# Attention and token-mixing on one core: eight changes in a hand-written order of steps

## The chip, the cores and the metric

The kernel runs on one core of a Trainium2 chip. The metric is the device time of one execution in microseconds (us); lower is better. A core has five engines that each work through their own list of instructions in order and meet only through semaphores: PE (TensorE, matrix products and transposes, with weight loads shown as PEld), DVE (VectorE), ACT (ScalarE), POOL (GpSimd) and SP (SyncE), which here only issues DMA transfers.

## What is computed

```python
# q, k, v: (8, 8, 576, 64) f32; per batch b and head h
r = relu(x);  phi(x) = concat([r * cos_w, r * sin_w], -1)      # 64 -> 128 features
kv  = einsum('bhsf,bhsd->bhfd', phi(k), v);  z = sum_s phi(k)
x   = (phi(q) @ kv) / (phi(q) @ z + 1e-6)                      # (8, 576, 512) with heads side by side
wq  = x @ w_q;  wk = x @ w_k                                   # (8, 576, 64)
W   = einsum('bsd,btd->bst', wq, wk) / 8
out = relu(einsum('bst,btd->bsd', W, x)) @ w_out               # (8, 576, 512) f32
```

The kernel computes the token mix as `wq @ (wk' x)`, so that the 576 x 576 matrix is never made.

## The kernel before

All work is cut into small named steps. A string, `ORDER`, lists some 650 of them, and a loop at the end of the kernel calls one function per word. The order on each engine is therefore the order of that engine's words in the list; nothing reorders it. The framework adds the waits between engines from the data that the steps read and write, on-chip memory banks included. SP's list is that of the loads (`LK`, `LQ`, `LV`, `LW`) and stores (`ST`): a store that waits for its data holds up every load written behind it.

A word is a step's name, a number, perhaps `a` or `b` for one half of it, `:n` for the PSUM bank, and `@A`, `@V` or `@G` for ACT, DVE or POOL. PSUM, the only memory that PE writes, has eight banks. Most steps write a pair, `n` and `n + 1`; `WK`, `WQ`, `KX` and `WO` write one. A step that writes a bank has to wait until the step that read the bank's former content is done. This reuse couples the engines most around the change.

The 64 (batch, head) pairs are worked on as 16 halves `H` of four heads (two pairs of heads each); a half gives two groups `g` = 2H and 2H + 1 (one head of each pair). For one half:

- `LK`, `LQ`, `LV` (line 145): load k, q and v, in parts a and b of 288 KB. Five buffers for each, so half 5 reuses those of half 0.
- `RK`, `RQ` (lines 203 and 205): relu and cast to bf16. `CV`, `VS` (lines 209 to 213 and 234) or, on POOL alone, `VG` (line 248): v times the cosine and sine tables.
- `QT` (wide: line 295, narrow: line 301) transposes q on PE: nine 128 x 128 transposes if the half is in `QT_WIDE`, else eighteen of 64 rows. `QM` (lines 316 and 320) multiplies the transposed q by the tables on DVE: two instructions for a wide half, one for a narrow one.
- `KV` (line 285, or wide: line 275) forms k'v with the sum of k in an extra column; `KE` copies it out of PSUM.
- `N` (line 340) is the numerator and denominator of one group; `EP`, `RC` or `RJ` and `X` (lines 357 to 393) divide and store x.
- `XT` (line 406) or `XR` (line 419) transposes x on PE, `XE` copies it out.

For a batch `b` of two halves: `WK` (line 439), `KW`, `WQ` (line 452), `QW`, `KX` (line 466), `XK` are the two projections and `wk' x`, with their copies; `XA` and `XB` copy one half of `wk' x` to the other 64 partitions, for each half of the channels. `MX` (line 489) gives the mixed tokens, four steps for a batch, and `ME` (lines 500 and 502) applies relu. Every nine `WO` (line 509) multiply two batches by w_out, 128 rows each; `OE` (lines 209 and 213) copies a result to one of 16 output buffers and `ST` (line 519) stores it.

In the trace all casts and copies of ACT have line 209, those of POOL line 211 and those of DVE line 213, so a row is matched with a step by its shape, its tile names and its place in the engine's order. For example the bank pairs around the two places in the middle read so:

```
PE: XR6:0 WO1:6 WO4:2 QT9:0 WK3:3 QT8:4 KV8:0 KV9:6 MX9:4 MX11:0 N16:2
PE: WO11:0 WO5:1 WO10:4 WO9:5 QT11:6 KV11:2 XR8:0 XR9:6 QT10:2 WO0:5 MX13:0 MX12:6 N22:2
PE: QT12:0 WO16:2 WO13:3 XR10:4 MX19:6 KV12:0 WO17:3 MX17:0 N25:6 N24:4
```

Of the kernel before, what the change touches and what calls it, by code (L numbers as in the profile page):

```python
# [26 lines left out]
LK1b TB TI LQ1a LQ0a TK LV1b TZ LV1a LK1a LQ1b TQ LQ0b LK0a RQ1a@G LV0a TW TV LV0b LK0b CV1@A LV3a
LV3b VS1b RQ1b@A LQ3b VS1a T2 QT1:0 LQ3a RK1a@A RK1b@V RQ0@V LK3b KV1:2 QM1 LK3a QT0:4 KE1@A CV0@G
LV2b RK0@A LW1 N2:2 VS0 N3:0 LQ2a LK2a VG3 QM0 KV0:6 LW0 KE0@A LV2a RC3 EP2@A X3 RQ3@A N0:6 N1:4
LQ2b RC2 EP0@V EP1@V X2 RK3@A LK2b QT3:0 RC0 XT1:2 LV5b X0 LV5a XE1@A RC1 X1 VG2b KV3:6 QM3 LK5b  # L30
XR0:4 KE3@A CW1@A N6:0 LK5a LQ5a XE0@V EP6@A N7:6 CW0@G LQ5b EP7@A WK0:4 VG2a RQ2@A LQ4b WQ0:5 KW0@V
RC6 LQ4a KX0:4 X6 RK2@A QT2:2 RC7 X7 CV5@A KV2:0 LK7a XK0@V LV4a QM2 XB0@G QW0@A XT3:6 LV4b KE2@A
RK5@A LK4a VS5a N5:0 WU5:2 LK4b N4:2 VS5b XE3@A RQ5@G LV7a EP5@V KV5:4 RC5 RC4 X5 XA0@A LV7b X4
QT5:6 KE5@A RQ4@G LQ7b MX0:0 QM5 XR2:2 ME0@A LQ7a QT4:4 XE2@A LQ6a N10:0 QM4 MX1:6 CV4@G LK7b EP10@A
ME1@A WK1:2 LV6b WQ1:3 RC10 KW1@A VS4 RK4@A LQ6b KX1:2 MX2:6 LW2 N11:4 XK1@V QW1@A ME2@A EP11@V
KV4:2 LK6b RC11 XA1@G X10 CV7a@A CV7b@G LK6a X11 MX5:6 MX4:0 KE4@A RQ7b@G LV6a RQ7a@A VS7 N8:2 N9:4
ME5@A LV8a ME4@A QT7:6 RK7@G LW3 EP8@V EP9@V RJ4 RQ6a@A XT5:0 X8 LW4 XB1@G XE5@A X9 KV7:2 LW5 RQ6b@G
QM7 LQ8b VG6b MX6:4 KE7@A XT4:0 LQ9b ME6@A MX7:2 XE4@V QT6:6 LV8b ME7@A N15:4 QM6 RK6a@A LQ8a MX3:2
N14:0 CV6a@G EP15@A RK6b@A WK2:6 LV9b ME3@A VS6a WQ2:7 LK8a KW2@A RC14 KV6:2 RC15 QW2@A LQ9a X14
CV8a@G KX2:7 LV9a KE6@A CW4@G X15 CW2@A N13:2 LK9a CW3@A CW5@V N12:0 EP13@V XR7:4 XK2@V LK8b WO8:6  # L40
RC13 XA2@A X13 EP12@A CV8b@G LK9b XE7@A WO2:7 RC12 VS8 LV11a WO7:2 CV9b@A RQ8a@G X12 OE8:0@A MX8:4
WO6:3 RQ8b@A RK8a@G LQ13a ME8@V OE7:1@A LQ11b XR6:0 RQ9a@G LQ10a WO1:6 CV9a@A XE6@V RQ9b@G LK11b
OE2:2@A WO4:2 LK11a VS9 OE6:3@A LQ11a RK8b@A QT9:0 RK9a@G OE1:4@A WK3:3 LV11b QM9 QT8:4 RK9b@G KW3@A
OE4:5@A KV8:0 QM8 XB2@A KV9:6 ST4 KE8@A LV12a MX9:4 KE9@A MX11:0 VG11a N16:2 ME9@A LK10a ME11@V
WQ3:6 RC16 LQ10b KX3:7 X16 QW3@A MX10:0 LV10a XK3@A N17:4 ME10@A N19:2 RK11@V N18:6 LV10b EP19@A
WO11:0 EP17@V RQ11@A LQ12a RC17 EP18@V X17 WO5:1 VG11b OE11:6@V WO10:4 OE5:5@A RC19 RC18 ST11 X18
WO9:5 LK12a X19 LK10b QT11:6 LQ13b OE9:7@A RQ10@G LV12b KV11:2 XA3@A QM11 XR8:0 LK12b KE11@A XR9:6
VG10a XE8@A QT10:2 LQ12b XE9@V WO0:5 QM10 OE10:8@A MX13:0 OE0:6@A MX12:6 N22:2 WO12:4 RQ13a@G ME12@V
EP22@A LV15a XB3@A ME13@A LV13a RC22 VG10b WK4:5 X22 LQ14b LV14b MX14:0 KW4@A N23:6 ME14@V LQ14a
MX15:2 EP23@A KX4:5 RK10@A LV13b WQ4:0 XK4@V RQ13b@G RC23 WO3:1 ME15@A X23 XA4@G XB4@A QW4@A RQ12b@G  # L50
KV10:2 OE3:9@V RQ12a@A QT13:6 OE12:10@A VG12 MX18:0 WO14:5 QM13 KE10@A ST12 ME18@A LK13b XR11:2
OE14:11@A LK13a MX16:0 N21:6 XE11@V ME16@A LV14a N20:4 EP21@A EP20@V RK12@A QT12:0 RJ10 X21 WO16:2
RQ14b@A X20 WO13:3 QM12 VG13 XR10:4 OE13:10@A MX19:6 KV12:0 ME19@A ST13 WO17:3 OE16:12@A LK15b
KE12@V XE10@V LK14b MX17:0 LK14a OE17:13@A N25:6 ME17@V N24:4 LV15b RQ14a@A WK5:3 ST2 EP25@V EP24@V
RK13@A RJ12 QT14:0 X24 WO21:2 KW5@A X25 CV14a@G KV13:4 OE21:10@A QM14 CV14b@A WQ5:3 ST21 KE13@A
# [2 lines left out]
ME23@A OE20:10@V XR13:4 RQ15a@G MX22:6 RQ15b@V MX20:0 ST20 ME22@A WO15:2 VG15a ST17 XE13@V ME20@A
ST8 N28:6 OE18:9@V OE15:14@A ST9 N29:0 EP28@A QT15:4 RK15@A EP29@V RC28 WK6:3 RC29 X29 WO25:2 KW6@A
QM15 WQ6:3 OE25:15@A KV15:0 X28 QW6@A ST25 ST7 KX6:3 KE15@A ST15 N31:0 ST18 XR14:6 EP31@V N30:4 ST0  # L60
XE14@V WO23:2 EP30@A ST10 XK6@A RJ15 ST16 X30 XA6@G WO24:3 ST5 OE23:7@A XB6@G X31 WO26:2 OE24:0@A
ST14 XR15:0 ST6 MX25:4 MX27:6 XE15@V ME25@A WO22:3 ST23 ME27@V ST1 WK7:0 OE26:9@V ST24 MX24:6 KW7@A
MX26:4 WQ7:1 ME24@A ME26@V ST19 KX7:0 OE22:8@V ST26 WO28:2 XK7@A QW7@V ST22 XA7@G WO27:3 OE28:11@A
XB7@G ST28 MX31:0 MX28:4 MX30:6 ME31@V ME28@A WO29:2 ME30@A OE27:7@V MX29:4 OE29:4@V WO30:0 ME29@A
ST27 ST29 WO32:1 OE30:2@V WO33:4 ST30 OE32:9@V WO34:0 ST32 OE33:8@A WO35:1 ST33 OE34:7@V WO31:4 ST34
OE35:4@A ST35 OE31:2@A ST31
"""


# [1 line left out]
def kernel(  # L71
# [240 lines left out]
    def QM(H, ps, eng):  # L312
        if H in QT_WIDE:
            q_t = qt_wide(place["QT", H]).rearrange("p c (r d) -> p r c d", r=2)
            for r in range(2):
                V.tensor_mul(  # L316
                    qm_b[H % NQM][:, :, r, 0:C, :],
                    q_t[:, r].unsqueeze(1).to_broadcast([P, 2, C, H2]), qtab)
# [280 lines left out]
```

## Time and profile before

| | |
|---|---|
| three runs | 119.94, 120.47, 120.84 us; median 120.47 |
| span of the profiled execution, first to last instruction | 117.9 us |
| its own time | not recorded beside the profile; the median is 2.57 us above its span |
| mean granted PE clock | 0.997 |
| busy: PE, DVE, ACT, POOL | 96.3, 91.0, 82.7, 64.8 us |
| moved by DMA | 39.38 MB, mean 334 GB/s |

An engine's busy time is the time in which at least one of its instructions was running. A row of a timeline gives start, duration, engine, source line, operation, output and inputs with their shapes, and the number of like instructions in a row that were merged; in brackets stands the time that the engine sat idle just before, and what released it, as far as the profile can infer it. The rows of PE overlap a little, since matmuls are pipelined and their ends are modelled; from start to start is the surer measure. Idle time on an engine that is not the bottleneck costs nothing.

### The profile page before, as it was taken

Reading aid. Unit: us, or ns where it says so; the run is one execution under the profiler, and the core shown is the slowest. Engines: PE = TensorE matmul, PEld = TensorE weight load, DVE = VectorE, ACT = ScalarE, POOL = GpSimd, SP = SyncE. Lnnn points to the kernel's source line nnn. Section 1 sums busy time; section 2 is a strip of 40 time slices with the busy share of each in tenths; the row PEclk is TensorE's granted clock in tenths of the full one; section 3 lists DMA queues with packets and bytes.
Section 4 is the critical chain, followed back from the end, with each engine's and each line's share of the span. In section 5 each row is a group of like instructions: output and inputs, shape, how many; then the busy total and the mean of one; then the engine's idle time right before and its main releaser. Section 6 shows DMA issues by size and latency. Waiting matters only on the chain.

```text
span 117.9 us, 4967 instructions
## 1 busy us (share of the span) xinstructions
PE 96.3 (82%) x2109; PEld 65.3 (55%) x2109; DVE 91.0 (77%) x163; ACT 82.7 (70%) x146; POOL 64.8 (55%) x66
## 2 busy tenths in 40 slices
PE   0007866887897879998999889997999999999970
PEld 0006855756676768546966556654784566463420
DVE  2009799699899998989798887796997996794620
ACT  4555578489999797997684769975888783546340
POOL 7600599843435984584599972899549921102000
PEclk9999999999999999999999999999999999999998
DMA  3999999999999999999999899786989456999874
GB/s 95 353 389 408 393 363 351 391 389 396 385 393 389 391 385 387 389 395 384 387 381 341 271 317 379 274 253 215 299 285 321 171 205 268 402 343 402 340 306 172
DMA packets 20662, 39.38 MB, mean 334 GB/s; under 512 B 3232, under 2 KB 3232, under 8 KB 20640
## 3 DMA queue, kind: packets, MB, share of 16 engines
q1 hardware_dynamic: 20640, 39.07, 91.8%
q8 instruction: 16, 0.26, 1.0%
q14 instruction: 6, 0.05, 0.1%
HBM read 29.62 MB, written 9.44 MB: 331 GB/s over the span
## 4 chain that ended last, share of the span: by engine, by line
PE 46%; DMA 25%; DVE 9%; SPq 8%; ACT 4%; issue 3%; POOL 2%; POOLq 0%; DVEq 0%
PE ps L509 23%; DMA kraw<-in_k_dram 11%; DMA vraw<-in_v_dram 9%; SPq L145 8%; DMA qraw<-in_q_dram 5%; DVE qm L316 5%; PE ps L340 4%; PE ps L452 3%; PE ps L466 3%; PE ps L489 3%; PE ps L439 3%; PE ps L285 3%; PE ps L419 2%; PE ps L295 2%; POOL rq L205 2%
## 5 line engine op out<-in xcount | busy, mean ns | idle before, releaser
L248 POOL TENSOR_TENSOR v<-vraw,vtab 128x1152 bf16<-128x1152 f32 (+1 forms) x12 | 35.6, 2976 | 4.5 <-DVE qm L316 2.5
L509 PE MATMUL ps<-wow,mix 128*128 128x512 bf16 x144 | 34.6, 380 | 0.0
L393 DVE TENSOR_TENSOR x<-ps,rec 128x640 bf16<-128x640 f32 x32 | 25.4, 816 | 0.7
L209 ACT COPY o<-ps 128x512 f32<-128x512 f32 x25 | 14.6, 590 | 10.5 <-PE ps L509 9.2
L316 DVE TENSOR_TENSOR qm<-ps,qtab 128x1152 bf16<-128x1152 bf16 x28 | 19.7, 749 | 1.3 <-PE ps L295 1.2
L509 PEld LDWEIGHTS <-mix 128*128 128x128 bf16 x144 | 12.5, 98 | 14.5 <-issue 1.7
L295 PE MATMUL ps<-ident,rq 128*128 128x128 bf16 x126 | 10.3, 232 | 10.9 <-ACT rq L203 10.0
L234 DVE TENSOR_TENSOR v<-vb,vtab 128x2304 bf16<-128x2304 bf16 (+1 forms) x11 | 12.0, 1110 | 7.5 <-ACT vb L209 6.7
L500 ACT ACTIVATE mix<-ps 128x576 bf16<-128x576 f32 x23 | 14.5, 651 | 2.5 <-PE ps L489 2.3
L340 PE MATMUL ps<-kvs,qm 64*128 64x65 bf16 x640 | 14.0, 193 | 2.8 <-DVE qm L316 1.8
L340 PEld LDWEIGHTS <-qm 64*128 64x128 bf16 x640 | 12.6, 96 | 4.9 <-issue 3.3
L295 PEld LDWEIGHTS <-rq 128*128 128x128 bf16 x126 | 8.2, 104 | 12.5 <-issue 9.9
L203 ACT ACTIVATE rk<-kraw 128x1152 bf16<-128x1152 f32 (+1 forms) x14 | 13.9, 995 | 0.5 <-DMA kraw<-in_k_dram 0.3
L211 POOL TENSOR_SCALAR kx<-kx 64x256 bf16<-64x256 bf16 x10 | 4.0, 400 | 15.8 <-ACT kx L209 10.1
L205 POOL TENSOR_SCALAR rq<-qraw 128x576 bf16<-128x576 f32 (+1 forms) x13 | 10.1, 776 | 4.4 <-ACT rk L203 2.6
L211 POOL TENSOR_SCALAR vb<-vraw 128x576 bf16<-128x576 f32 (+1 forms) x7 | 5.7, 809 | 10.8 <-DMA vraw<-in_v_dram 9.5
L285 PE MATMUL ps<-v,rk 64*64 64x130 bf16 x432 | 9.1, 228 | 1.9 <-ACT mix L500 0.7
L209 ACT CAST kvs<-ps 128x260 bf16<-128x260 f32 (+1 forms) x15 | 6.5, 436 | 5.1 <-PE ps L285 3.8
L285 PEld LDWEIGHTS <-rk 64*64 64x64 bf16 x432 | 7.5, 112 | 4.3 <-ACT mix L500 1.3
L502 DVE TENSOR_SCALAR mix<-ps 128x576 bf16<-128x576 f32 x9 | 6.8, 753 | 3.3 <-PE ps L489 3.1
L213 DVE COPY xT<-ps 128x1280 bf16<-128x1280 bf16 (+1 forms) x9 | 7.3, 813 | 2.2 <-PE ps L419 2.0
L203 ACT ACTIVATE rq<-qraw 128x576 bf16<-128x576 f32 (+1 forms) x10 | 8.3, 830 | 0.9 <-DMA qraw<-in_q_dram 0.8
(65 smaller groups left out, 135.0 us busy)
## 6 DMA issues: line engine op xcount, KB each, us to landing
kraw<-in_k_dram SPq DMA_DIRECT2D x32, 288.0 KB, 5.9
qraw<-in_q_dram SPq DMA_DIRECT2D x32, 288.0 KB, 5.9
vraw<-in_v_dram SPq DMA_DIRECT2D x32, 288.0 KB, 5.9
out_dram<-o SPq DMA_DIRECT2D x36, 256.0 KB, 3.0
wof<-in_moe_w_out_dram SPq DMA_DIRECT2D x4, 256.0 KB, 5.7
wkf<-in_moe_w_k_dram SPq DMA_DIRECT2D x1, 128.0 KB, 6.7
wqf<-in_moe_w_q_dram SPq DMA_DIRECT2D x1, 128.0 KB, 6.5
```

Source lines behind the costliest of these rows:

```text
L203: A.activation(dst, s, AF.Relu)
L205: eng.tensor_scalar(dst, s, FMAX, 0.0, op0=ALU.min, op1=ALU.max)
L209: A.copy(dst, s)
L234: V.tensor_mul(v2_b[H % NV2][:, part, :, :, 0:D], vb_b[H % NPREP][:, part].unsqueeze(3).to_broadcast([P, n, C, 2, D]), vtab.unsqueeze(1).t ...
L248: G.tensor_mul(dst[:, part, :, :, 0:D], s[:, part].unsqueeze(3).to_broadcast([P, n, C, 2, D]), vtab.unsqueeze(1).to_broadcast([P, n, C, 2, ...
L285: nc.tensor.matmul(kv_v[o, r, :], rk_of(H)[a, pr, c, :], v2_b[H % NV2][a, pr, c, :, 0:D + 1], start=(c == 0), stop=(c == C - 1))
L295: nc.tensor.transpose(qt_v[:, c, :], rq_b[H % NPREP][:, c, :, :], ident)
L316: V.tensor_mul(qm_b[H % NQM][:, :, r, 0:C, :], q_t[:, r].unsqueeze(1).to_broadcast([P, 2, C, H2]), qtab)
L340: nc.tensor.matmul(nv[:, pr, u, :], qm_b[H % NQM][a, s, r, 2 * u:2 * u + 2, :], kv_b[H % 2][a, r, pr if H in KV_WIDE else 0, s, 0:D + 1], ...
L393: V.tensor_tensor(x_b[b % NX][:, :, 4 * h:4 * h + 4, :].rearrange("p u (w r) d -> p r w u d", r=2)[:, r], nv[:, :, :, 0:D], rec(g).to_broa ...
L500: A.activation(dst, s, AF.Relu, scale=scale_moe)
L509: nc.tensor.matmul(o, mix_b[bp % 2][:, m, rt * P:(rt + 1) * P], wow[:, m, :], start=(m == 0), stop=(m == NDM - 1))
```

## The change

`ORDER` is written anew, and almost every line of the list differs, since loads and stores stand in other columns between the same neighbours of their own queue. What matters is each engine's own order. There it does the following; DVE's order stays as it is.

```diff
 SP
-LQ0b LK0a LV0a LV0b LK0b LV3a
+LQ0b LV0a LV0b LK0b LK0a LV3a
 PE
-XR6:0 WO1:6 WO4:2 QT9:0 WK3:3 QT8:4 KV8:0
+XR6:0 WO1:6 QT8:4 QT9:0 WK3:3 WO4:2 KV8:0
...
-WO11:0 WO5:1 WO10:4 WO9:5 QT11:6 KV11:2 XR8:0 XR9:6 QT10:2
+WO11:0 WO5:1 QT11:4 WO9:0 WO10:1 KV11:2 XR8:6 XR9:4 QT10:2
...
-XR10:4 MX19:6 KV12:0 WO17:3
+XR10:4 KV12:6 MX19:0 WO17:3
...
-WO25:2 WQ6:3 KV15:0 KX6:3 N31:0
+WO25:2 KV15:0 KX6:3 WQ6:2 N31:0
 ACT
-QW1@A ME2@A CV7a@A KE4@A
+QW1@A ME2@A XA1@A CV7a@A KE4@A
...
-OE25:15@A QW6@A KE15@A EP30@A
+OE25:15@A KE15@A QW6@A EP30@A
 POOL
-CV4@G XA1@G CV7b@G
+CV4@G CV7b@G
```

The other edit is in the list of the wide halves, which half 12 leaves:

```diff
-    QT_WIDE = (0, 1, 2, 3, 4, 5, 6, 7, 8, 9, 10, 11, 12, 14)
+    QT_WIDE = (0, 1, 2, 3, 4, 5, 6, 7, 8, 9, 10, 11, 14)
```

So half 0's first part of k is loaded three places later; two q transposes stand ahead of output products, one k'v ahead of a mix product, and with them the banks of seven steps are exchanged; one projection stands behind `wk' x`; one small copy changes its engine; and the transposes of half 12 are eighteen narrow ones, with one `QM` instruction instead of two.

More of the change, by code (lines that the diff above doesn't have):

```diff
@@ L26 @@
 ORDER = """
[L27 to L55, printed above, removed]
@@ L56 @@
-KX5:2 LQ15b VS14 LQ15a XR12:4 XK5@A N27:0 ST3 XE12@A N26:6 LK15a RK14a@G WO20:2 RC26 EP27@V RC27
-XA5@G RK14b@A X27 WO19:4 XB5@G QW5@A VG15b X26 KV14:0 OE19:2@A MX21:6 KE14@A MX23:4 WO18:3 ME21@V
[L58 to L66, printed above, removed]
+LK1b LQ1a LQ0a LV1b LV1a LK1a LQ1b LQ0b LV0a LV0b LK0b LK0a LV3a LV3b LQ3b LQ3a LK3b LK3a LV2b LW1
@@ new lines @@
+LQ2a LK2a LW0 LV2a LQ2b LK2b TB TI TK TZ TQ RQ1a@G TW TV CV1@A VS1b RQ1b@A VS1a T2 QT1:0 RK1a@A
+RK1b@V RQ0@V KV1:2 QM1 QT0:4 KE1@A CV0@G LV5b LV5a RK0@A LK5b LK5a LQ5a LQ5b LQ4b LQ4a N2:2 VS0 N3:0
+VG3 QM0 KV0:6 KE0@A RC3 EP2@A X3 RQ3@A N0:6 N1:4 RC2 EP0@V EP1@V X2 RK3@A QT3:0 RC0 XT1:2 X0 XE1@A
+RC1 X1 VG2b KV3:6 QM3 XR0:4 KE3@A CW1@A N6:0 XE0@V EP6@A N7:6 CW0@G EP7@A WK0:4 VG2a RQ2@A WQ0:5
+KW0@V RC6 KX0:4 X6 RK2@A LK7a LV4a LV4b LK4a LK4b LV7a LV7b LQ7b LQ7a LQ6a LK7b LV6b LQ6b LW2 LK6b
+LK6a LV6a LV8a LW3 LW4 LW5 LQ8b QT2:2 RC7 X7 CV5@A KV2:0 XK0@V QM2 XB0@G QW0@A XT3:6 KE2@A RK5@A
@@ new lines @@
+VS5a N5:0 WU5:2 N4:2 VS5b XE3@A RQ5@G EP5@V KV5:4 RC5 RC4 X5 XA0@A X4 QT5:6 KE5@A RQ4@G LQ9b LV8b
+LQ8a MX0:0 QM5 XR2:2 ME0@A QT4:4 XE2@A N10:0 QM4 MX1:6 CV4@G LV9b LK8a LQ9a LV9a EP10@A ME1@A WK1:2
+WQ1:3 RC10 KW1@A VS4 RK4@A LK9a LK8b LK9b KX1:2 MX2:6 N11:4 XK1@V QW1@A ME2@A EP11@V KV4:2 XA1@A
+RC11 X10 CV7a@A CV7b@G X11 MX5:6 MX4:0 KE4@A RQ7b@G RQ7a@A VS7 N8:2 N9:4 ME5@A ME4@A QT7:6 RK7@G
+EP8@V EP9@V RJ4 RQ6a@A XT5:0 X8 XB1@G XE5@A X9 KV7:2 RQ6b@G QM7 VG6b MX6:4 KE7@A XT4:0 ME6@A MX7:2
+XE4@V QT6:6 ME7@A N15:4 QM6 RK6a@A MX3:2 N14:0 CV6a@G LV11a EP15@A RK6b@A WK2:6 ME3@A VS6a WQ2:7
@@ new lines @@
+KW2@A RC14 KV6:2 RC15 QW2@A X14 CV8a@G KX2:7 KE6@A CW4@G X15 CW2@A N13:2 CW3@A CW5@V N12:0 EP13@V
+XR7:4 XK2@V WO8:6 RC13 XA2@A X13 EP12@A CV8b@G XE7@A WO2:7 RC12 VS8 WO7:2 CV9b@A RQ8a@G LQ13a LQ11b
+LQ10a LK11b LK11a LQ11a LV11b X12 OE8:0@A MX8:4 WO6:3 RQ8b@A RK8a@G ME8@V OE7:1@A XR6:0 RQ9a@G WO1:6
+CV9a@A XE6@V RQ9b@G OE2:2@A QT8:4 VS9 OE6:3@A RK8b@A QT9:0 RK9a@G OE1:4@A WK3:3 QM9 WO4:2 RK9b@G
+KW3@A OE4:5@A ST4 LV12a LK10a LQ10b LV10a LV10b LQ12a KV8:0 QM8 XB2@A KV9:6 KE8@A MX9:4 KE9@A MX11:0
@@ new lines @@
+VG11a N16:2 ME9@A ME11@V WQ3:6 RC16 KX3:7 X16 QW3@A MX10:0 XK3@A N17:4 ME10@A N19:2 RK11@V N18:6
+EP19@A WO11:0 EP17@V RQ11@A RC17 EP18@V X17 WO5:1 VG11b OE11:6@V ST11 LK12a LK10b LQ13b LV12b LK12b
+LQ12b QT11:4 OE5:5@A RC19 RC18 X18 WO9:0 X19 WO10:1 OE9:7@A RQ10@G KV11:2 XA3@A QM11 XR8:6 KE11@A
+XR9:4 VG10a LV15a LV13a LQ14b LV14b LQ14a LV13b XE8@A QT10:2 XE9@V WO0:5 QM10 OE10:8@A MX13:0
+OE0:6@A MX12:6 N22:2 WO12:4 RQ13a@G ME12@V EP22@A XB3@A ME13@A RC22 VG10b WK4:5 X22 MX14:0 KW4@A
+N23:6 ME14@V MX15:2 EP23@A KX4:5 RK10@A WQ4:0 XK4@V RQ13b@G RC23 WO3:1 ME15@A X23 XA4@G XB4@A QW4@A
@@ new lines @@
+RQ12b@G KV10:2 OE3:9@V RQ12a@A QT13:6 OE12:10@A ST12 LK13b LK13a LV14a VG12 MX18:0 WO14:5 QM13
+KE10@A ME18@A XR11:2 OE14:11@A MX16:0 N21:6 XE11@V ME16@A N20:4 EP21@A EP20@V RK12@A QT12:0 RJ10 X21
+WO16:2 RQ14b@A X20 WO13:3 QM12 VG13 XR10:4 OE13:10@A ST13 LK15b LK14b LK14a LV15b ST2 KV12:6 MX19:0
+ME19@A WO17:3 OE16:12@A KE12@V XE10@V MX17:0 OE17:13@A N25:6 ME17@V N24:4 RQ14a@A WK5:3 EP25@V
+EP24@V RK13@A RJ12 QT14:0 X24 WO21:2 KW5@A X25 CV14a@G KV13:4 OE21:10@A ST21 LQ15b LQ15a ST3 LK15a
+QM14 CV14b@A WQ5:3 KE13@A KX5:2 VS14 XR12:4 XK5@A N27:0 XE12@A N26:6 RK14a@G WO20:2 RC26 EP27@V RC27
@@ new lines @@
+XA5@G RK14b@A X27 WO19:4 XB5@G QW5@A VG15b X26 KV14:0 OE19:2@A MX21:6 KE14@A MX23:4 WO18:3 ME21@V
+ME23@A OE20:10@V ST20 ST17 ST8 ST9 XR13:4 RQ15a@G MX22:6 RQ15b@V MX20:0 ME22@A WO15:2 VG15a XE13@V
+ME20@A N28:6 OE18:9@V OE15:14@A N29:0 EP28@A QT15:4 RK15@A EP29@V RC28 WK6:3 RC29 X29 WO25:2 KW6@A
+QM15 OE25:15@A ST25 ST7 ST15 ST18 ST0 ST10 ST16 ST5 ST14 ST6 KV15:0 X28 KX6:3 KE15@A WQ6:2 N31:0
+XR14:6 EP31@V QW6@A N30:4 XE14@V WO23:2 EP30@A XK6@A RJ15 X30 XA6@G WO24:3 OE23:7@A ST23 ST1 XB6@G
+X31 WO26:2 OE24:0@A ST24 ST19 XR15:0 MX25:4 MX27:6 XE15@V ME25@A WO22:3 ME27@V WK7:0 OE26:9@V ST26
@@ L67 @@
+MX24:6 KW7@A MX26:4 WQ7:1 ME24@A ME26@V KX7:0 OE22:8@V ST22 WO28:2 XK7@A QW7@V XA7@G WO27:3
+OE28:11@A ST28 XB7@G MX31:0 MX28:4 MX30:6 ME31@V ME28@A WO29:2 ME30@A OE27:7@V ST27 MX29:4 OE29:4@V
+ST29 WO30:0 ME29@A WO32:1 OE30:2@V ST30 WO33:4 OE32:9@V ST32 WO34:0 OE33:8@A ST33 WO35:1 OE34:7@V
+ST34 WO31:4 OE35:4@A ST35 OE31:2@A ST31
 """
```

## The prediction

> **What bounds the kernel now.** I read the view by windows first, then the chain that ended last, then the timelines of each engine around the places that the change touches. A window's row gives its length and the busy time of PE, PEld (weight loads), DVE, ACT and POOL, with the number of instructions in brackets, then granted clock, DMA share and GB/s.
>
> ```profile
> span 117.9 us, 4967 instructions
> ```
> ```profile
> 0.00:31.28 31.28, 17.50 (x455) 14.17 (x455) 21.30 (x45) 20.84 (x32) 17.71 (x26) 1.00 0.99 354
> 31.28:44.18 12.90, 10.94 (x257) 9.15 (x258) 12.61 (x23) 11.93 (x22) 8.11 (x9) 1.00 1.05 390
> 44.18:56.01 11.83, 11.40 (x218) 7.30 (x218) 10.54 (x19) 10.10 (x20) 6.62 (x9) 1.00 1.05 389
> 56.01:68.75 12.74, 11.77 (x297) 8.22 (x297) 10.95 (x21) 8.72 (x17) 11.18 (x6) 1.00 0.99 344
> 68.75:80.67 11.92, 11.11 (x251) 7.08 (x251) 9.94 (x16) 10.20 (x21) 8.56 (x6) 1.00 0.85 291
> 80.67:114.30 33.63, 33.59 (x633) 19.39 (x633) 25.66 (x44) 20.35 (x38) 12.67 (x12) 1.00 0.84 300
> ```
>
> Three regimes. Up to 31.28 the DMA share is 0.99 while PE is busy for 17.50 of 31.28 us: loads set the pace. The chain says the same:
>
> ```profile
> 23.57 6.34 DMA qraw<-in_q_dram
> ...
> 30.07 1.16 POOL rq L205
> ```
>
> A load of q lands at 29.9, POOL makes RQ4 from it, and only then does PE run QT4. From 44.18 to 80.67 PE is short of busy by 0.43 + 0.97 + 0.81 = 2.21 us, in a few waits. From 80.67 to the last product PE is idle for 0.04 us: whatever brings PE's instruction at 81 forward should bring the end forward by as much.
>
> **The change part by part.** Beside the re-wrapped list, each engine's own order changes in few places; DVE's does not change at all.
>
> *A. QT8 goes ahead of QT9, and WO4 behind WK3.* PE, DVE and ACT today:
>
> ```profile
> 52.10 1.90 PE L509 MATMUL ps<-wow,mix 128*128 128x512 bf16 x8
> 53.83 0.67 PE L295 MATMUL ps<-ident,rq 128*128 128x128 bf16 x9
> ...
> 56.01 1.25 PE L285 MATMUL ps<-v,rk 64*64 64x130 bf16 x72 [0.43 <-DVE qm L316]
> 57.34 0.42 PE L489 MATMUL ps<-wq,kx 64*128 64x288 bf16 x4
> ```
> ```profile
> 52.95 1.35 DVE L234 TENSOR_TENSOR v<-vb,vtab 128x2304 bf16<-128x2304 bf16 x1
> 54.54 2.75 DVE L316 TENSOR_TENSOR qm<-ps,qtab 128x1152 bf16<-128x1152 bf16 x4 [0.24 <-PE ps L295]
> ```
> ```profile
> 55.44 0.59 ACT L209 COPY o<-ps 128x512 f32<-128x512 f32 x1
> ```
>
> WO1 and WO4 take 53.83 - 52.10 = 1.73, so 0.87 each by their starts. KV8 (56.01) waits until QM9, the first half of the DVE row at 54.54, has read the banks of QT9. Without WO4 ahead of them QT8 starts at 52.97 and QT9, half a microsecond later, is done near 54.1, so QM9 waits for nothing but VS9, which ends at 52.95 + 1.35 = 54.30. That is 0.24 sooner. WK3 and WO4 then fill PE's wait until about 55.5. MX9 needs all of QM8 (54.54 + 2.75 = 57.29, MX9 at 57.34), so it too comes 0.24 sooner. **Gain 0.24**, between 0 (if QT8 has to wait at its new place) and the whole wait of 0.43. The cover that goes: OE4, on ACT at 55.44, now finds WO4 just done, so it may begin 0.1 to 0.2 later, and ST4 with it, and behind ST4 in SP's queue six loads (LV12a to LQ12a). They feed RQ10, VG10 and RQ12, of which QT10, a good 9 us on, is the first needed. I take 0 for that.
>
> *B. QT11 goes ahead of WO9 and WO10; banks of QT11, WO9, WO10, XR8 and XR9 change.*
>
> ```profile
> 60.39 3.63 PE L509 MATMUL ps<-wow,mix 128*128 128x512 bf16 x16
> 63.86 0.67 PE L295 MATMUL ps<-ident,rq 128*128 128x128 bf16 x9
> ...
> 66.04 0.47 PE L419 MATMUL ps<-ident,x 64*128 64x64 bf16 x20 [0.47 <-DVE qm L316]
> ...
> 68.75 0.48 PE L340 MATMUL ps<-kvs,qm 64*128 64x65 bf16 x20 [0.42 <-DVE qm L316]
> ```
> ```profile
> 62.46 1.56 DVE L393 TENSOR_TENSOR x<-ps,rec 128x640 bf16<-128x640 f32 x2
> 64.56 1.42 DVE L316 TENSOR_TENSOR qm<-ps,qtab 128x1152 bf16<-128x1152 bf16 x2 [0.54 <-PE ps L295]
> 66.54 0.82 DVE L213 COPY xT<-ps 128x1280 bf16<-128x1280 bf16 x1 [0.56 <-PE ps L419]
> 67.28 1.41 DVE L316 TENSOR_TENSOR qm<-ps,qtab 128x1152 bf16<-128x1152 bf16 x2
> ```
> ```profile
> 60.39 1.15 ACT L203 ACTIVATE rq<-qraw 128x1152 bf16<-128x1152 f32 x1
> ...
> 66.73 0.59 ACT L209 COPY o<-ps 128x512 f32<-128x512 f32 x1
> ```
>
> DVE waits 0.54 for QT11, XR9 waits 0.47 for QM11 (64.56 + 1.42 = 65.98, XR9 at 66.04: 0.06 from release to start), and N22 at 68.75 waits for QM10. With A the stage starts 0.24 sooner. Two products later, at 60.15 + 1.74 = 61.89, QT11 starts; RQ11 on ACT is done at 61.54 at the latest. QM11 now waits only for X18 and X19 (62.46 + 1.56 = 64.02, less 0.24 = 63.78) and is done at 65.20. PE meanwhile runs QT11, KV11 and XR8, which take 66.04 - 0.47 - 63.86 = 1.71, and WO9 and WO10, 1.74, until 65.34; so XR9 starts there without a wait, 0.70 before today's 66.04. From XR9 on the chain is today's: XE9 after it, QM10 after that, N22 at 68.75 - 0.70 = 68.05. **Gain 0.46 more**, 0.70 in all. New waits: WO0 shares a bank with XR9 and stands until XE9 has read it, near 66.7, which the wait for QM10 covers. MX13 shares a bank with WO10 and needs OE10, queued on ACT behind XE8; OE10 ends today at 67.32, and MX13 is now reached near 67.6. No cost, but with 0.3 us of margin. Bounds: 0.3 (one of the two waits stays) to 0.89 (0.47 + 0.42).
>
> *C. KV12 goes ahead of MX19, with banks exchanged; QT12 is narrow.*
>
> ```profile
> 77.05 0.66 PE L295 MATMUL ps<-ident,rq 128*128 128x128 bf16 x9
> ...
> 80.67 0.72 PE L285 MATMUL ps<-v,rk 64*64 64x130 bf16 x36 [0.71 <-ACT mix L500]
> 81.32 1.04 PE L509 MATMUL ps<-wow,mix 128*128 128x512 bf16 x4
> ```
> ```profile
> 94.15 0.42 PE L301 MATMUL ps<-ident,rq 64*128 64x64 bf16 x18
> ```
> ```profile
> 77.64 1.55 DVE L393 TENSOR_TENSOR x<-ps,rec 128x640 bf16<-128x640 f32 x2
> 79.11 1.41 DVE L316 TENSOR_TENSOR qm<-ps,qtab 128x1152 bf16<-128x1152 bf16 x2
> ```
> ```profile
> 74.34 9.09 POOL L248 TENSOR_TENSOR v<-vraw,vtab 128x2304 bf16<-128x2304 f32 x2 [0.39 <-PE ps L285]
> ```
>
> The view blames ACT for the 0.71 before KV12. But KV12 writes the banks of QT12, and QM12, which reads them, ends at 79.11 + 1.41 = 80.52; I read the wait as QM12's. In the new order KV12 (banks 6 and 7, free once X21 is done) runs in that wait, and MX19, two matmuls, takes the wait over. QM12 still follows X20 on DVE: with 0.70 from A and B it ends at 79.82, MX19 runs at 79.88, and WO17 at about 80.03 (0.15 for two matmuls, an estimate from the four at 57.34) against 81.32. **Gain 0.59 more, 1.29 in all.** KV12 also needs VG12, the first half of POOL's row: 74.34 + 9.09 / 2 = 78.89, less what KV10 brings forward. PE gets there near 78.9 (80.67, less the wait of 0.71, MX19 and the 0.70, and less the saving of QT12): at worst 0.1, covered by the wait before MX19. Bounds: 0.2 to 0.72, KV12's whole time.
>
> The narrow QT12 takes 18 transposes: QT15 is so made today, 0.42 beside 0.66 for the wide one, 0.24 less. But the wait before MX19 is DVE's, so it is worth 0 (0 to 0.24). The Trainium skill, TensorEngine Tiling (Array Packing), section Key Properties, says that a change of tiling mode drains TensorE, and a narrow transpose between 128-row products adds such changes. It gives no price; QT15's row, which has matmuls of other shapes on both sides, already holds whatever it costs here, so by the rule the sum stays.
>
> *D. XA1 goes from POOL to ACT, ahead of CV7a.*
>
> ```profile
> L209 ACT COPY kx<-kx 64x256 bf16<-64x256 bf16 x6 | 2.4, 403 | 0.3 <-DVE kx L213 0.2
> ```
> ```profile
> 35.68 0.67 ACT L209 CAST vb<-vraw 128x576 bf16<-128x576 f32 x1
> 36.50 0.59 ACT L209 CAST kvs<-ps 128x520 bf16<-128x520 f32 x1
> ```
> ```profile
> 37.15 0.80 PE L340 MATMUL ps<-kvs,qm 64*128 64x65 bf16 x40 [0.44 <-ACT kvs L209]
> ```
> ```profile
> 36.87 1.60 DVE L234 TENSOR_TENSOR v<-vb,vtab 128x2304 bf16<-128x2304 bf16 x1
> ```
>
> It puts 0.40 into ACT ahead of KE4 at 36.50, less the 0.15 that ACT stood before KE4: N8 and N9 end at 38.2 instead of 37.95. Their first reader on DVE stands behind VS7, which ends at 36.87 + 1.60 = 38.47. Hidden: 0, at worst 0.40; POOL is rid of a wait, which at best ends VS7 0.2 sooner.
>
> *E. LK0a goes behind LV0a, LV0b, LK0b.*
>
> ```profile
> 12.59 1.16 ACT L203 ACTIVATE rk<-kraw 128x1152 bf16<-128x1152 f32 x1 [0.33 <-DMA kraw<-in_k_dram]
> ```
>
> RK0 needs both halves of k; the last is still the twelfth load. v of half 0 lands one load sooner, so VS0 may gain some tenths, but RQ4 waits for its own load at 29.9, whose place is the same. 0 (-0.2 to +0.2).
>
> *F. WQ6 goes behind KX6, KE15 ahead of QW6.* In the last window but the tail PE is never idle, so there is no wait to remove: 0.
>
> **Sum.** 0.24 + 0.46 + 0.59 = 1.29 us. The profiled span is 117.9; the runs' median is 120.47, so 2.57 lie around the span, which I keep. New span 116.6, time 120.47 - 1.29 = 119.2.
>
> **Rivals.**
>
> 1. *ACT keeps the middle where it is: 119.9.*
>
> ```profile
> 71.53 1.15 ACT L203 ACTIVATE rk<-kraw 128x1152 bf16<-128x1152 f32 x1
> ```
>
> ACT works nearly without a break from RK10 at 71.53 until PE reaches KV12's wait. If RK10 can't start sooner, for its load or for what stands before it, the gain of A and B dies there and C's 0.59 stays. For it: 10.20 of 11.92 busy. Against: just ahead ACT waits for PE, and PE would be early.
>
> 2. *Nothing decisive moves: 120.4.* DVE's order is unchanged, and if it is DVE rather than the order on PE that spaces QM9, QM11 and QM12, the waits reappear beside other instructions. Against: DVE itself waits 0.24, 0.54 and 0.56 for PE at A and B.
>
> 3. *All waits go: 118.3.* The 2.21 of idle between 44.18 and 80.67 vanish. Against: MX19's new wait.
>
> 4. *Slower: QT8 isn't ready at its new place: 120.9.* PE is in order. Should QT8 be able to start only at its present time, near 54.9, PE idles from 52.97, and WO4 no longer fills: MX9 waits until both halves of QM, 2.75, have followed QT8 and QT9, near 58.8 instead of 57.34. That is 1.5 lost against 1.05 from B and C: 0.45 slower. It decides once QT8 starts later than about 54.5. Against: RQ8 and RQ9 stand in ACT's and POOL's queues well ahead of 53; only the order seems to hold QT8.
>
> **How the numbers follow.** Chances: forecast 0.48, rival 1 0.22, rival 2 0.10, rival 3 0.12, rival 4 0.08. About 1% (1.2 us) can be told from no change. Faster by over 1% means below 119.27: about 0.29 of the forecast's 0.48, whose centre lies just beyond that bound, all of rival 3's and a little of rival 1's: 0.45. Slower by over 1% is the far end of rival 4: 0.06. The rest, 0.49, lies within 1%. Range 118.2 to 120.6: from rival 3 to just short of rival 4, with 0.15 outside; the forecast's own range is 118.7 to 119.7.
>
> **What would show it.** Right: KV8 waits under 0.25; the waits at XR9 (0.47) and N22 (0.42) are gone; KV12 starts at once and MX19 waits some 0.3 for QM12; the final products end near 113.0 instead of 114.3. Wrong: a wait before QT8 or QT11, MX13 waiting for OE10, KV12 waiting for VG12, QT7 or KV7 late near 38 to 40, or a PE that comes early to 82 and then waits for k of half 14.

## The result, and the profile after

The median of four runs went from 120.66 us (119.94 to 120.85) to 118.83 us (118.42 to 119.22): a ratio of 0.986, 95% interval 0.982 to 0.990. The forecast was 119.2, and the span it gave, 116.6, is the one measured. The profiled execution took 118.42 us in all, so 1.8 us lie around its span. Executions of one kernel fall into a usual group and a slower one; ratios compare the usual ones, while the profiles of D alone, of C with half 12 wide, of the changed kernel with XA1 on POOL and of its second run below are of slower ones.

The page, and the view by windows cut at the same steps as the prediction's (QT4, WK2, KV8, N22, KV12, the last product's end). Columns: window, length, then busy time and instructions of PE, PEld, DVE, ACT and POOL, granted clock, DMA share, GB/s.

```profile
span 116.6 us, 4971 instructions
```
```profile
0.00:31.50 31.50, 17.23 (x455) 14.16 (x455) 21.27 (x45) 20.81 (x32) 17.61 (x26) 1.00 0.99 354
31.50:44.66 13.16, 10.93 (x257) 9.13 (x258) 12.44 (x23) 12.34 (x23) 8.01 (x8) 1.00 1.05 388
44.66:56.16 11.50, 11.30 (x216) 7.20 (x218) 10.39 (x19) 9.70 (x20) 6.99 (x9) 1.00 1.05 388
56.16:68.26 12.10, 11.60 (x294) 8.09 (x296) 10.79 (x20) 8.78 (x17) 8.78 (x5) 1.00 0.95 322
68.26:79.17 10.91, 10.44 (x258) 6.92 (x258) 9.16 (x15) 9.66 (x20) 9.95 (x7) 1.00 0.95 343
79.17:113.00 33.83, 33.22 (x634) 19.55 (x635) 26.50 (x45) 21.24 (x40) 13.42 (x12) 1.00 0.83 303
```

Three windows are shorter: by 0.33 (11.83 to 11.50), 0.64 (12.74 to 12.10) and 1.01 (11.92 to 10.91). Of the last, 0.45 is no gain: KV12, at which the window ends, now stands ahead of MX19, and from KV12 to WO17 it takes 1.10 instead of 0.65. The first is longer by 0.22 (loads), the last by 0.20 (it now holds MX19), and the second, which the prediction left alone, by 0.26. The clock is 1.00 throughout.

PE of the changed kernel, at A, B, C and the end. Columns: start, duration, engine, line, operation, tiles, shapes, count, and in brackets the idle time before it with its releaser.

```profile
52.57 1.04 PE L509 MATMUL ps<-wow,mix 128*128 128x512 bf16 x4
53.45 1.17 PE L295 MATMUL ps<-ident,rq 128*128 128x128 bf16 x18
...
56.16 1.24 PE L285 MATMUL ps<-v,rk 64*64 64x130 bf16 x72
57.49 0.42 PE L489 MATMUL ps<-wq,kx 64*128 64x288 bf16 x4
...
60.54 1.90 PE L509 MATMUL ps<-wow,mix 128*128 128x512 bf16 x7
62.28 0.67 PE L295 MATMUL ps<-ident,rq 128*128 128x128 bf16 x9
...
65.25 0.76 PE L419 MATMUL ps<-ident,x 64*128 64x64 bf16 x40
...
66.93 1.02 PE L509 MATMUL ps<-wow,mix 128*128 128x512 bf16 x3 [0.31 <-DVE xT L213]
...
68.26 0.49 PE L340 MATMUL ps<-kvs,qm 64*128 64x65 bf16 x20
...
79.17 0.72 PE L285 MATMUL ps<-v,rk 64*64 64x130 bf16 x36
80.03 0.30 PE L489 MATMUL ps<-wq,kx 64*128 64x288 bf16 x2
80.27 1.04 PE L509 MATMUL ps<-wow,mix 128*128 128x512 bf16 x3
...
107.65 5.35 PE L509 MATMUL ps<-wow,mix 128*128 128x512 bf16 x24
```

The brackets of the old kernel before KV8, XR9, N22 and KV12 are gone. QT8 and QT9 run as one row of 18, and XR8 and XR9 as one row of 40. The wait that takes their place is the one foretold, 0.31 before WO0 for XE9's bank; MX19's, foretold as some 0.3, is 0.21 (80.03 is 0.86 behind KV12's start, and KV12 took 0.65 from start to start before). The last product ends at 107.65 + 5.35 = 113.00.

### The profile page after: what moved, and what is told of

Same layout as the page of the kernel before. It is cut to its first block, busy times and chain, and to the rows that moved or that the text cites. A ratio compares the mean times of both kernels' runs of the same rounds, so it can differ in the third digit from the quotient of the medians.

```text
span 116.6 us, 4971 instructions
## 1 busy us (share of the span) xinstructions
PE 94.7 (81%) x2104; PEld 65.1 (56%) x2118; DVE 90.5 (78%) x162; ACT 83.1 (71%) x147; POOL 64.8 (56%) x65
## 4 chain that ended last, share of the span: by engine, by line
PE 48%; DMA 26%; DVE 14%; SPq 4%; issue 3%; ACT 1%; DVEq 0%; ACTq 0%
PE ps L509 24%; DMA qraw<-in_q_dram 16%; DMA vraw<-in_v_dram 5%; DMA kraw<-in_k_dram 5%; PE ps L340 5%; DVE qm L316 5%; SPq L145 4%; PE ps L285 3%; PE ps L489 3%; PE ps L419 3%; PE ps L439 3%; DVE xT L213 3%; PE ps L466 3%; PE ps L452 2%; DVE x L393 2%
## 5 line engine op out<-in xcount | busy, mean ns | idle before, releaser
L509 PE MATMUL ps<-wow,mix 128*128 128x512 bf16 x130 | 33.3, 380 | 1.2 <-issue 0.3
L295 PE MATMUL ps<-ident,rq 128*128 128x128 bf16 x117 | 9.5, 233 | 12.0 <-ACT rq L203 11.0
L316 DVE TENSOR_TENSOR qm<-ps,qtab 128x1152 bf16<-128x1152 bf16 x26 | 18.3, 749 | 0.8 <-PE ps L295 0.7
L295 PEld LDWEIGHTS <-rq 128*128 128x128 bf16 x117 | 7.6, 104 | 13.6 <-issue 10.5
```

What stands on the lines that cost most here:

```text
L295: nc.tensor.transpose(qt_v[:, c, :], rq_b[H % NPREP][:, c, :, :], ident)
L316: V.tensor_mul(qm_b[H % NQM][:, :, r, 0:C, :], q_t[:, r].unsqueeze(1).to_broadcast([P, 2, C, H2]), qtab)
L509: nc.tensor.matmul(o, mix_b[bp % 2][:, m, rt * P:(rt + 1) * P], wow[:, m, :], start=(m == 0), stop=(m == NDM - 1))
```

## The experiments

The runs' scatter (119.9 to 120.9 us over four runs of one kernel) is as large as most single edits, so I read each edit first in its own stage, from start to start on PE, and then in the time. In the table a row of letters is the kernel before plus those parts. "KV4 to WK2" is where D should act, "WK2 to WO11" A, "WO11 to N22" B, "N22 to WO17" C and "WO25 to N31" F; a star marks a stage in which PE paused in the middle of a step (last section). Stages that the table leaves out have pauses too, which the text names.

| kernel | KV4 to WK2 | WK2 to WO11 | WO11 to N22 | N22 to WO17 | WO25 to N31 | ratio to before (95%) |
|---|---|---|---|---|---|---|
| before | 8.91 | 16.21 | 8.36 | 12.57 | 2.89 | 1 |
| after | 9.23 | 15.88 | 7.72 | 12.01 | 2.77 | 0.986 (0.982 to 0.990) |
| A | 8.92 | 15.88 | 8.35 | 12.58 | 2.89 | 0.993 (0.990 to 0.996) |
| B | 8.92 | 16.32* | 7.77 | 12.66* | 2.89 | 0.991 (0.987 to 0.995) |
| C | 8.92 | 16.21 | 8.35 | 12.05* | 2.89 | 0.990 (0.986 to 0.994) |
| C, half 12 wide | 8.92 | 16.32* | 8.76* | 12.07 | 2.89 | 0.996 (0.992 to 0.999) |
| D | 9.23 | 16.21 | 8.36 | 13.52* | 2.89 | 1.000 (0.996 to 1.003) |
| E | 8.93 | 16.21 | 8.35 | 12.83* | 2.89 | 0.996 (0.993 to 0.9995) |
| F | 8.92 | 16.21 | 8.35 | 12.58 | 2.76 | 0.999 (0.995 to 1.003) |
| A, B, C | 8.92 | 15.88 | 7.72 | 12.01 | 2.88 | 0.987 (0.983 to 0.990) |
| A, B, C, F | 8.93 | 15.88 | 7.72 | 12.00 | 2.76 | 0.986 (0.981 to 0.991) |
| after, XA1 on POOL | 8.93 | 15.88 | 7.72 | 14.61* | 2.76 | 0.989 (0.984 to 0.994) |
| after, a second time | 9.19 | 15.88 | 7.72 | 12.16* | 2.76 | 0.988 (0.984 to 0.992) |

The theory was the prediction's sum: A, B and C act each at its own place, their gains add up, and nothing else matters. The rivals: the gains die in the next stage, or one part carries them all.

**A, B and C, each alone.**

```diff
 A, PE
-WO4:2 QT9:0 WK3:3 QT8:4 KV8:0
+QT8:4 QT9:0 WK3:3 WO4:2 KV8:0
 B, PE
-WO11:0 WO5:1 WO10:4 WO9:5 QT11:6 KV11:2 XR8:0 XR9:6
+WO11:0 WO5:1 QT11:4 WO9:0 WO10:1 KV11:2 XR8:6 XR9:4
 C, PE, and half 12 out of QT_WIDE
-MX19:6 KV12:0
+KV12:6 MX19:0
```

> Kernel before with place A alone (QT8 ahead of QT9, WO4 behind WK3). The measure is the time on PE from QT4 (31.28 before) to the first of the last 24 product matmuls (108.91): 77.63 before, 76.15 after. Theory of the places (each wait taken from PE is passed on to the end, and they add up): 77.3, that is 0.3 less, and ratio near 0.997. Rival, absorption (what A gives is taken back at the waits before XR9, N22 and KV12, which DVE sets): 77.6, ratio 1.000.

> Kernel before with place B alone (QT11 ahead of WO9 and WO10, with the banks of the five steps). Theory of the places: the waits at XR9 (0.47) and N22 (0.42) are gone, a wait of some 0.3 before WO0 comes up, 77.0 from QT4 to the last products, 0.6 less, ratio near 0.995. Rival, absorption: N22 comes early but KV12 still stands until QM12 is done at the old time; 77.5, ratio 0.999.

> Kernel before with place C alone (KV12 ahead of MX19 with banks exchanged, half 12 narrow). Theory of the places: KV12 starts without a wait, 77.05 from QT4 to the last products, 0.55 to 0.6 less, ratio near 0.995. Rival: MX19 takes over the whole wait of 0.7 and only the time of the two matmuls moves; 77.5, ratio 0.999.

Each shortens its own stage and no other: A by 0.33, B by 0.59, C by 0.52; the other stages are as before to about 0.1, but for B's from WO17 to WO25, 14.08 instead of 13.78.

The measure named ahead, from QT4 to the first of the last 24 product matmuls, says less: 77.19 for A, 77.70 for B and 77.22 for C, where before takes 77.63. B missed its 77.0 and even the rival's 77.5. In its trace PE pauses at matmuls 989, 1373 and 1628 (last section), which adds 0.1 to the stage before its own, 0.1 to the next and 0.3 to the one from WO17 to WO25, and QT4 to KV4 takes 0.15 longer; without these it would be 77.0. So B's gain is read from its own stage alone.

With A alone PE still shows B's and C's waits:

```profile
65.88 0.47 PE L419 MATMUL ps<-ident,x 64*128 64x64 bf16 x20 [0.47 <-DVE qm L316]
...
68.59 0.49 PE L340 MATMUL ps<-kvs,qm 64*128 64x65 bf16 x20 [0.42 <-DVE qm L316]
...
80.52 0.72 PE L285 MATMUL ps<-v,rk 64*64 64x130 bf16 x36 [0.72 <-ACT mix L500]
```

So the three waits are independent, and none needs another's earlier start. The times agree in sign and order but say more: A, B and C alone gain 0.69%, 0.92% and 0.97%, together 3.1 us, where the stages give 1.4 us and the three in one kernel 1.6 us. The excess, some half a microsecond for each kernel, is in no stage of their traces; what I can say of it stands in the last section.

**D alone, and the changed kernel without it.**

```diff
 ACT, D alone
-QW1@A ME2@A CV7a@A KE4@A
+QW1@A ME2@A XA1@A CV7a@A KE4@A
 POOL
-CV4@G XA1@G CV7b@G
+CV4@G CV7b@G
```

The other kernel is the changed one with these lines put back.

> Kernel before with D alone (XA1 on ACT). As predicted, hidden: 77.6, WK2 13.0 after QT4 (44.18 less 31.28 is 12.90 before), ratio 1.000. Theory from the trace after, where WK2 starts 13.16 after QT4 and VS7 half a microsecond later: ACT is on the path at 36 to 39 and D costs 0.25; 77.9, ratio 1.002. If it is D, VS7 on DVE waits here too; if the 0.25 came from a load that landed late in that one run, VS7 does not wait.

> Kernel after with D alone undone: XA1 back on POOL. Theory: ACT is on the path at 36 to 39, so D costs 0.3: from KV4 to N8 1.88 as before (after: 2.19), VS7 on DVE does not wait, and the time from QT4 to the last nine products (72.64 after) falls to 72.35, ratio near 0.983. Rival, D as predicted is hidden and the late WK2 came from the loads of that run: 72.6, ratio as after, 0.986.

In the times D doesn't show: 1.000, and 0.989 without it beside 0.986 with it, intervals overlapping. In the trace it does: KV4 to WK2 takes 9.19 to 9.23 in the three traces with D and 8.91 to 8.93 in the eleven others. **D costs 0.3 us.** ACT, then DVE, then PE of the changed kernel, DVE with D alone, and last RQ7b on POOL before and in the changed kernel:

```profile
35.97 0.40 ACT L209 COPY kx<-kx 64x256 bf16<-64x256 bf16 x1
36.40 0.67 ACT L209 CAST vb<-vraw 128x576 bf16<-128x576 f32 x1
36.98 0.59 ACT L209 CAST kvs<-ps 128x520 bf16<-128x520 f32 x1
```
```profile
37.59 1.36 DVE L234 TENSOR_TENSOR v<-vb,vtab 128x2304 bf16<-128x2304 bf16 x1 [0.42 <-ACT kvs L209]
38.86 0.24 DVE L359 TENSOR_SCALAR rec<-ps 128x10 f32<-128x10 f32 x2
```
```profile
37.62 0.80 PE L340 MATMUL ps<-kvs,qm 64*128 64x65 bf16 x40 [0.76 <-ACT kvs L209]
```
```profile
37.76 1.36 DVE L234 TENSOR_TENSOR v<-vb,vtab 128x2304 bf16<-128x2304 bf16 x1 [0.48 <-ACT kvs L209]
```
```profile
36.60 0.67 POOL L205 TENSOR_SCALAR rq<-qraw 128x576 bf16<-128x576 f32 x1
```
```profile
36.27 0.67 POOL L205 TENSOR_SCALAR rq<-qraw 128x576 bf16<-128x576 f32 x1
```

XA1 (35.97) moves CV7a from 35.68 to 36.40, and CV7a writes a part of `vb`, which VS7 reads. DVE, which had no gap there, now stands 0.42 before VS7. The view names KE4's `kvs` as the releaser, but VS7 doesn't read `kvs`: its input from ACT is CV7a's, and in the kept trace DVE's queue passes VS7's wait for ACT at 37.11, right behind CV7a's end (36.40 + 0.67 = 37.07). VS7 starts 0.46 after that wait, and in none of the fourteen traces less than 0.44 after it. What fills this stretch no row shows; before, it lay under X11 on DVE.

Behind VS7 stands RC8, which reads N8, and behind RC8 the next 6 us of DVE's work. After KV4, VS7 starts 0.56 later than before, and RC8 only 0.3, since VS7 takes 1.36 instead of 1.60. That comes from POOL. In each of the eleven traces with XA1 on POOL, RQ7b is still running there when VS7 starts, for 0.26 to 0.40 us, and VS7 takes 1.21 us plus that time, to within 0.01 (before: 36.60 + 0.67 - 36.87 = 0.40). With XA1 on ACT, RQ7b is done at 36.94. QT7 on PE, which waits for ACT's ME4, comes 0.3 later too, but behind it PE stands 0.32 for DVE's x before and after, so DVE's road is the longer one.

The windows say the same of the stage: DVE was idle for 12.90 - 12.61 = 0.29 before and for 13.16 - 12.44 = 0.72 now.

**A, B and C together; C with half 12 wide.** The first is the three diffs above in one kernel; the second is C's diff without the edit of `QT_WIDE`.

> Kernel before with A, B and C and nothing else. Theory, the places add up: the sum of the three alone in the traces is 0.33 + 0.59 + 0.52 = 1.44, so from QT4 to WO28 74.13 - 1.44 = 72.7 at the most, ratio near 0.985. Rival, a part of one place's gain is waited away at the next: 73.2, ratio 0.990.

> Kernel before with KV12 ahead of MX19 and their banks exchanged, half 12 still wide. From N22 to WO17 before takes 12.57, with both parts of C 12.05. Theory, MX19 waits for QM12 on DVE, so the narrow transposes are hidden: 12.1. Rival, the narrow half 12 brings its own 0.24 on PE: 12.3.

The three add up without loss: 15.88, 7.72 and 12.01, the changed kernel's own stages. The measure named ahead, from QT4 to WO28, is 73.31 all the same, nearer the rival's 73.2 than 72.7: from WO17 to WO25 this trace takes 14.51 where the changed kernel takes 13.69, with a pause of PE inside KV14 (last section). Half 12 made narrow is worth at most 0.06 (12.07 wide; narrow 12.01 with A and B, and 12.05 alone, with a pause in it), and by so much QM12 is shorter as one instruction (1.35 beside 1.41). The ratios, 0.990 and 0.996, differ by more than that, but their intervals meet at 0.992 to 0.994, so I leave that open rather than call it an effect of the narrow transposes.

**MX19 later still: a version that failed.** In the changed kernel MX19 still waits some 0.2 for QM12. This kernel is the changed one with XA1 on POOL, OE16 ahead of ME19 on ACT, and

```diff
 PE
-KV12:6 MX19:0 WO17:3 MX17:0 N25:6 N24:4
+KV12:6 WO17:3 MX19:0 N25:6 MX17:0 N24:4
```

> Kernel after with XA1 on POOL and, behind KV12, the order WO17, MX19, N25, MX17, N24 in place of MX19, WO17, MX17, N25, N24. Theory: the wait that MX19 took over (PE stands some 0.3 between KV12 and MX19) is now filled by WO17; from N22 to XR12 17.35 instead of 17.68, ratio near 0.981. Rival: ACT and DVE, whose relu and divisions come later, set the pace there: 17.7, ratio as with XA1 on POOL.

```profile
79.43 0.72 PE L285 MATMUL ps<-v,rk 64*64 64x130 bf16 x36
80.08 1.04 PE L509 MATMUL ps<-wow,mix 128*128 128x512 bf16 x4
81.05 0.30 PE L489 MATMUL ps<-wq,kx 64*128 64x288 bf16 x2
81.18 0.47 PE L340 MATMUL ps<-kvs,qm 64*128 64x65 bf16 x20
82.09 0.30 PE L489 MATMUL ps<-wq,kx 64*128 64x288 bf16 x2 [0.43 <-ACT mix L500]
```

MX19's wait is gone, and MX17 has one twice as long. It shares MX19's bank and needs ME19 to have read it; with only N25 between them that is 0.43 too early. KV12 to XR12 takes 7.14 instead of 6.77, and the ratio is 0.991 (0.988 to 0.995). From N22 to XR12, the stretch named ahead, it takes 18.64 where 17.35 was forecast and the changed kernel takes 17.68; 0.59 of this last difference lies ahead of KV12, behind a pause of PE at matmul 1373. A wait moved on, not removed.

**E alone, F alone.**

```diff
 SP, E
-LQ0b LK0a LV0a LV0b LK0b LV3a
+LQ0b LV0a LV0b LK0b LK0a LV3a
 PE and ACT, F
-WO25:2 WQ6:3 KV15:0 KX6:3 N31:0        OE25:15@A QW6@A KE15@A EP30@A
+WO25:2 KV15:0 KX6:3 WQ6:2 N31:0        OE25:15@A KE15@A QW6@A EP30@A
```

> Kernel before with E alone (LK0a behind LK0b). Theory, hidden: CV0 on POOL comes some 0.7 sooner after QT1 (2.32 before), N0 some 0.3 sooner after QT1 (6.24 before), but RQ4 waits for its own load, so QT4 stays within 31.1 to 31.7 and the ratio is 1.000. Rival: the gain in the head reaches the end; QT4 at 31.0 or less, ratio 0.997.

> Kernel before with F alone (WQ6 behind KX6). Prediction on record: 0, for PE is never idle there. Theory from the trace after: no wait goes, but the same matmuls stand beside other shapes and take 0.12 less (WO25 to N31 2.77 instead of 2.89), ratio 0.999. If F only moves the work, 2.89.

E does bring v of half 0 sooner: POOL's first cast, 2.32 after QT1 before, is 1.56 after it here, and N0 is 5.44 instead of 6.24 after QT1. Then it is lost at RQ4, which waits for its own load (POOL with E alone):

```profile
11.40 1.15 POOL L211 TENSOR_SCALAR vb<-vraw 128x1152 bf16<-128x1152 f32 x1 [6.39 <-DMA vraw<-in_v_dram]
...
29.98 1.15 POOL L205 TENSOR_SCALAR rq<-qraw 128x1152 bf16<-128x1152 f32 x1 [0.37 <-DMA qraw<-in_q_dram]
```

QT4 starts at 31.18, and in the kernels without E between 30.79 and 32.18. The ratio's interval ends at 0.9995, so a small gain elsewhere isn't excluded; no stage shows one.

F's stage is 0.12 shorter in every kernel that has it, without any wait in it. PE before, then with F alone:

```profile
95.10 1.03 PE L509 MATMUL ps<-wow,mix 128*128 128x512 bf16 x4
96.06 0.68 PE L452 MATMUL ps<-xT,wqw 128*64 128x288 bf16 x8
96.67 0.72 PE L285 MATMUL ps<-v,rk 64*64 64x130 bf16 x36
97.32 0.74 PE L466 MATMUL ps<-x,wk 128*64 128x256 bf16 x10
97.99 0.48 PE L340 MATMUL ps<-kvs,qm 64*128 64x65 bf16 x20
```
```profile
95.80 0.72 PE L285 MATMUL ps<-v,rk 64*64 64x130 bf16 x36
96.45 0.74 PE L466 MATMUL ps<-x,wk 128*64 128x256 bf16 x10
97.02 0.66 PE L452 MATMUL ps<-xT,wqw 128*64 128x288 bf16 x8
97.61 0.48 PE L340 MATMUL ps<-kvs,qm 64*128 64x65 bf16 x20
```

From start to start KX6 took 0.67 ahead of N31 (64\*128) and takes 0.57 ahead of WQ6, which has its own tile shape, 128\*64. One change of tile shape less, 0.1 us less.

**A, B, C and F, without D and E; and the changed kernel again.**

> Kernel before with A, B, C and F, without D and E, as the candidate for a faster version than the change as given. Theory: without D it saves 0.3 against the kernel after; from QT4 to WO28 72.35 where the kernel after took 72.64, and, beside the kernel after on the same chip, a median lower by 0.3 us. Rival: D and E cost nothing that reaches the end; 72.6 and no difference.

> The kernel after once more, on the chip of the three others, so that they can be compared with it. All theories: the ratio on record, 0.982 to 0.990, and from KV4 to N8 2.19. Its spread shows what part of a difference of 0.3 us can be told from chance.

From QT4 to WO28 this kernel takes 72.35 us, the changed one 72.64 and the old one 74.13: the 0.3 of D is won back, and its span, 116.4, is 0.2 below the changed kernel's. (The changed kernel with XA1 on POOL should have shown 72.35 as well and took 75.50, with three pauses of PE.) By time the two can't be told apart (medians 118.79 and 119.03, ratios 0.986 and 0.988, intervals overlapping), so it is the better kernel by its trace only.

## Why the prediction was right, step by step

- **A: right, undersized.** 0.33 instead of 0.24. QM9 now follows VS9 at once (DVE 53.43, then 54.69, in the rows below): 1.26 from start to start, while I had added VS9's whole 1.35. Neighbours on DVE overlap by about 0.1 in these rows, so QM9 starts that much before VS9's row ends. The lost cover was sized right: OE4 begins at 56.10 (row below), which is 11.44 after WK2 (44.66) where it was 11.26 before (55.44 less 44.18), 0.18 later, and ST4 and the loads behind it move with it. It stayed free: QT10 follows XR9 without a gap.
- **B: right, undersized.** 0.64 instead of 0.46, for the same reason (X19 at 62.61, QM11 at 64.08: 1.47, not 1.56) and because PE takes 3.28 from QT11 to XR9 where I charged 3.45: QT11 takes 0.50 from start to start (62.28 to 62.78) and not 0.59, and XR8 0.31 and not the 0.47 of its whole row, while WO9 and WO10 take 0.08 more. XR9's and N22's waits are both gone, which the lower bound of 0.3 had left open, and MX13 has no wait.

OE4 on ACT, and DVE, of the changed kernel; DVE's gaps before QM9 and QM11 (0.24 and 0.54) are gone:

```profile
56.10 0.59 ACT L209 COPY o<-ps 128x512 f32<-128x512 f32 x1 [0.44 <-PE ps L509]
```

```profile
53.43 1.35 DVE L234 TENSOR_TENSOR v<-vb,vtab 128x2304 bf16<-128x2304 bf16 x1
54.69 2.75 DVE L316 TENSOR_TENSOR qm<-ps,qtab 128x1152 bf16<-128x1152 bf16 x4
...
62.61 1.56 DVE L393 TENSOR_TENSOR x<-ps,rec 128x640 bf16<-128x640 f32 x2
64.08 1.41 DVE L316 TENSOR_TENSOR qm<-ps,qtab 128x1152 bf16<-128x1152 bf16 x2
```

- **C: right.** 0.56 instead of 0.59. KV12 starts at once, MX19 takes a shorter wait over, and the narrow transposes are worth nothing, since the wait is QM12's.
- **D: wrong.** The step that failed is "Their first reader on DVE stands behind VS7, which ends at 36.87 + 1.60 = 38.47. Hidden: 0, at worst 0.40". VS7 was no cover of its own: the same insertion delays it through CV7a, by 0.56. The 0.2 that the prediction allowed for POOL is there, 0.24 in VS7's length, and the price that is left is 0.3, inside the bounds.
- **E: right** as far as the stages show. **F: wrong by 0.12.** "There is no wait to remove: 0" looked for idle time only; the saving is in how long busy matmuls take beside others. The Trainium skill, TensorEngine Tiling (Array Packing), section Key Properties, says that a change of tiling mode drains TensorE. The prediction weighed that rule for QT12, where nothing hung on it, and not for F, where F's stage agrees with it at about 0.1 us for one change.
- **The sum.** From KV4 to WO28 the stages give +0.32 (D), -0.33, -0.64, -0.56, -0.12 (F) and -0.09 between WO17 and WO25, which is before's own: its trace pauses for 0.08 at matmul 1628 (last section), and those of A alone and F alone, which don't, are as much shorter: -1.42, and 70.14 - 68.71 = 1.43 is measured. KV4 itself starts 0.16 later (loads), so WO28 comes 1.27 sooner, and the span is 1.3 shorter. The prediction's 1.29 was thus right in part by cancellation, that is by luck: A, B and F brought 0.39 more than foretold, D and the start took 0.48.
- **2.57 around the span: wrong.** Every run for which both are listed has 1.7 to 1.9. The profiled execution of before, 117.9, was one of its shortest: in the three groups of runs beside the experiments its lowest spans were 117.8 to 118.0, its median ones 118.4 to 118.8. That is why the medians differ by 1.83 and the two traces by 1.3; the interval, 1.2 to 2.2 us, holds both.
- **The rivals.** ACT doesn't keep the middle, and DVE doesn't space it (the gains pass to the end undiminished); QT8 starts at 53.45 without a wait, so the slower case never began; not all waits went (0.31 before WO0, some 0.2 before MX19).

## What to carry to other kernels

Work that hides a delay must be traced to its own inputs: if the delayed engine also feeds the cover, the cover moves too. A product put between a producer and a consumer on an in-order engine is free only where the consumer's engine waits anyway, so look for the gap on the other engine (DVE's 0.24 and 0.54 here) and check the bank's next writer before you count it as won. An edit without a wait to remove can still save time on PE if it brings equal tile shapes together, and edits of 0.1 to 0.6 us are read in stages from start to start, not in runs that scatter by 1 us.
